# Weight conversions stepped in fewer phases of a pass, and another order of the seven products of a group

## The chip, the cores and the metric

The kernel runs on one core of a Trainium2 chip. The metric is the device time of one execution in microseconds (us). Three runs of the kernel before took 1336.34, 1339.28 and 1339.46 us; the median is 1339.28 us. The engines are called as the profile calls them: PE multiplies matrices (PEld is its weight load), DVE, ACT and POOL work element by element, SP issues the DMAs.

## The reference

Attention over 4 batches of 448 rows and 12 heads of 64, with a normalisation of q and k, and then two feed-forward layers, each of which takes 768 features to 2048 and back. The weights of the layers come as float64.

```
attn   = softmax(rms(q)*g_q @ (rms(k)*g_k).T / 8) @ v       # 4 x 12 x 448 x 64
x      = attn, heads put side by side                        # 1792 x 768
h      = x @ w1_in;  g = s * relu(h)**2 + b;  x = g @ w1_out
h      = x @ w2_in;  g = h * cos(h);          out = g @ w2_out
```

## The kernel before

**The stages.** Attention, and beside it the first layer for batches 0 and 1, fill the first 590 us or so. Then come three passes: the first layer for batches 2 and 3, called (0, 1), the second layer for batches 0 and 1, (1, 0), and for batches 2 and 3, (1, 1). A pass has eight groups p = 0 to 7 (`NCK`), each of 256 of the 2048 hidden features. `phase_in` of a group makes the hidden values, `phase_out` multiplies them with the out-weights and adds to an accumulator. The phases stand in the order in 0, in 1, out 0, in 2, out 1, ..., in 7, out 6, out 7, so that only the first two in-phases of a pass follow each other without an out-phase between them.

**Three matmuls for one product.** Every operand is held as a high and a low part (`halves`, L379: ACT rounds the high part, POOL or DVE subtracts it to get the low one), and `products` (L100) multiplies high by high, low by high and high by low.

**The seven products of a group.** `phase_in` (L743) computes four quarters of the hidden values, two blocks of features by two batches, with seven products instead of eight; sums and differences of weights (`s1` to `s4`, made by `prepare_in`, L685) and of inputs (`1` to `4`, made by `prepare_x`, once for a pass) take the place of the eighth. Each product is 9 matmuls of 128x448 (L763), 63 for a group. Four PSUM banks, a, b, c and d, hold the results:

1. a takes `11` x `11`; ACT copies it out (`p1`, L779).
2. b takes `s2` x `2`; DVE makes `u2` = b + p1 (L767).
3. c takes `s3` x `3`; DVE makes `u3` = c + u2 (L767).
4. d takes `s1` x `1`; DVE adds u3 and writes the quarter (1, 1) to b (L772), and its epilogue starts.
5. a takes on `12` x `21`: quarter (0, 0), no sum needed.
6. c takes on `22` x `4`; DVE adds u2 (L772): quarter (1, 0).
7. d takes on `s4` x `22`; DVE adds u2 (L772): quarter (0, 1).

Product 6 has to wait until u3 has read bank c, product 7 until L772 has read bank d. The epilogue of a quarter (L468 to L483) works in its bank and ends with `gl` (L483) on DVE; only then is the bank free. The next group's four banks are given out in the order in which the group before frees them.

**The conversion of weights.** `convert` (L385) turns one 128x384 piece of float64 weights into float32: SP loads it into one of two `raw` buffers (384 KB), ACT makes `c` and `t` (L402, L403), DVE needs three instructions (L407, L406, L408), SP stores it (L411). The raw buffer is free when L406 has read it. The second layer has 64 such pieces (`pieces`). In passes (0, 1) and (1, 0) every step of a phase adds a fixed rate to a credit (`conversion`, L825), and a piece is converted for each whole credit.

**What sets the order.** The code is written as generators that are stepped side by side, but a scheduler then sets the order of the instructions on each engine by its own timeline: an instruction may stand far ahead of its place in the code if its operands are there. Each engine then works through its list in that order, so an instruction that waits holds up all behind it on its engine.

**Names.** In rows of the order, `u_u2_0_1_6` is u2 of group 6 of pass (0, 1), `ph_1_0_0_a` bank a of group 0 of pass (1, 0), `xr_1_1_...` an input of `prepare_x` for pass (1, 1), `acc` the accumulator (L532 in the first layer, L556 in the second), `c_1_1_7_1_1` and `t_1_1_7_1_1` the working tiles of a converted piece. The DVE's u2 of a group is used as a mark below: "mark 6" is u2 of group 6 of pass (0, 1).

Of the kernel before, what the change touches and what calls it, by code (L numbers as in the profile page):

```python
# [33 lines left out]
def body(ctx, tc, q, k, v, g_q, g_k, w1_in, w1_out, s_in, b_in, w2_in, w2_out, out):  # L34
# [11 lines left out]
    NCK = NF // CF  # L46
# [53 lines left out]
    def products(w, x):  # L100
        return ((w[0], x[0]), (w[1], x[0]), (w[0], x[1]))
# [268 lines left out]
    def tile_of(ck, f):  # L370
        return ck + NCK * f

    def block(key):
        n = count["block"]
        count["block"] += 1
        pool, bufs = (pools["lt"], 5) if "lt" in pools and n % 11 > 5 else (wp, 6)
        return [pool.tile([P, CW], F32R, tag=f"w{z}", name=f"w{z}_{key}", bufs=bufs) for z in "hl"]
# [46 lines left out]
    def recall(key, parts):  # L424
        for z, d in zip(parts, ready[key]):
            nc.sync.dma_start(z.bitcast(F32), d)
# [256 lines left out]
            yield  # L683

    def prepare_in(layer, pr, p):  # L685
        names = ("11", "s2", "s3", "s1", "12", "22", "s4")
        w = late_w["in", layer, pr, p] = {z: block(f"{layer}_{pr}_{p}_{z}") for z in names}
        if (layer, pr) == (1, 1):
            for z in names:
                recall((p, z), w[z])  # L690
                yield
            return

        def fetch(what, f, k):
            nc.sync.dma_start(what, fetched(layer, 0, tile_of(p, f), 0, k))
            return what

        def f32(what):
            return pools["lt"].tile([P, CW], F32, tag="tf", name=f"tf_{layer}_{pr}_{p}_{what}", bufs=4)

        def operand(what, t):
            halves(t, *w[what])
            if layer == 1:
                store((p, what), w[what])

        a11, a22, a12 = (fetch(w[z][1].bitcast(F32), *at) for z, at in (("11", (0, 0)), ("22", (1, 1)), ("12", (0, 1))))
        a21 = fetch(f32("21"), 1, 0)
        yield
        s1, s2 = f32("s1"), f32("s2")
        nc.gpsimd.tensor_tensor(s1, a21, a22, ALU.add)  # L710
        nc.gpsimd.tensor_tensor(s2, s1, a11, ALU.subtract)
        yield
        nc.gpsimd.tensor_tensor(a21, a11, a21, ALU.subtract)
        operand("11", a11)
        yield
        operand("s2", s2)
        yield
        nc.gpsimd.tensor_tensor(s2, a12, s2, ALU.subtract)
        operand("s3", a21)
        yield  # L720
        operand("s1", s1)
        yield
        operand("12", a12)
        yield
        operand("22", a22)
        operand("s4", s2)
        yield
# [15 lines left out]
    def phase_in(layer, pr, p):  # L743
# [12 lines left out]
        def bank(what):  # L756
            return pools["psb"].tile([P, 512], F32, tag="ph", name=f"ph_{key}_{what}", bufs=4)[:, :S]

        def product(at, a, b, first):
            wb = [z.rearrange("p (c f) -> p c f", f=P) for z in w[a]]  # L760
            for c in range(NE // 2):
                for n, (z, m) in enumerate(products([z[:, c, :] for z in wb], x[b, c])):
                    nc.tensor.matmul(at, z, m, start=(first and c == 0 and n == 0), stop=(c == NE // 2 - 1 and n == 2), skip_group_check=not first)  # L763
# [6 lines left out]
        def result(f, b, h, u=None, into=None):  # L770
            if u is not None:
                nc.vector.tensor_tensor(into, h, u, ALU.add)  # L772
                h = into
            epilogue_in_bank(layer, f"{key}_{f}_{b}", h, *(z[:, b, :] for z in pairs[f]))

        pa = bank("a")
# [5 lines left out]
        product(pb, "s2", "2", True)  # L782
        u2 = combine("u2", pb, p1)
        yield
        pc = bank("c")
        product(pc, "s3", "3", True)
        u3 = combine("u3", pc, u2)
# [1 line left out]
        pd = bank("d")  # L789
        product(pd, "s1", "1", True)  # L790
        result(1, 1, pd, u3, pb)
        yield
        product(pa, "12", "21", False)
        result(0, 0, pa)
        yield
        product(pc, "22", "4", False)
        result(1, 0, pc, u2, pc)
# [20 lines left out]
    def fetched(*key):  # L818
        while key not in plain:
            convert(*pieces.pop(0), late=True)  # L820
        return plain[key]
# [3 lines left out]
    def conversion(rate):  # L825
        credit[0] += rate
        while pieces and credit[0] >= 1:
            credit[0] -= 1
            convert(*pieces.pop(0), late=True)
# [45 lines left out]
    passes = [(0, 1), (1, 0), (1, 1)]  # L875
# [12 lines left out]
    for n, (phase, *at) in enumerate(phases):  # L888
        behind = [prepared(phases[n + 1])] if n + 1 < len(phases) else []
        q_, p = tuple(at[:2]), at[2]  # L890
        later = passes[passes.index(q_) + 1:]
        if later and p == NCK - 2 and phase is phase_out:
            soon = [prepare_x(*later[0])]
        for _ in phase(*at):
            for z in behind:
                next(z, None)
            for z in soon:
                next(z, None)
                next(z, None)
            if q_ != passes[-1]:  # L900
                conversion(6 / 13 if q_ == passes[0] else 2.3 / 14)
        for z in behind:
            for _ in z:
                pass
# [28 lines left out]
```

## Time and profile before

| | |
|---|---|
| median of three runs | 1339.28 us |
| the profiled execution | 1341.06 us, of which the span 1339.3 us |
| PE busy in the span | 1231.5 us (92%) |
| DVE busy in the span | 976.0 us (73%) |
| ACT, POOL busy | 778.6 us (58%), 576.5 us (43%) |
| mean granted clock of PE | 0.965 |
| first matmul of pass (0, 1) after a wait | 594.19 us |
| mark 0 and mark 6 of pass (0, 1) on DVE | 617.41 and 792.65 us |
| the first group of pass (1, 0), its u2 | 873.9 us |

A line of a timeline gives the start, the duration, the engine, the line of the kernel, the operation with its output and inputs, and in square brackets the time that the engine had been idle and what ended it. A line of groups gives the busy time in us, the mean of one in ns, and behind the bar the idle time just before such instructions. Matmuls are pipelined, so the time from start to start, not the printed duration, is what one costs.

### The profile page before, as it was taken

The numbers are of one execution on the slowest core, as the hardware profiler recorded it, in microseconds if no ns is written. First come the engines' busy times: TensorE is split into PE (matmuls) and PEld (weight loads), VectorE is DVE, ScalarE is ACT, GpSimd is POOL, SyncE is SP. The second block draws the span as 40 slices with busy tenths as digits, with TensorE's granted clock in tenths as the row PEclk, the third lists the DMA queues.
The fourth block names the chain that finished last, engine by engine and source line by source line (L and its number), as shares of the span: only waits on it lengthen the run. The fifth ranks groups of instructions, "written<-read, shape, count | busy, mean of one in ns | idle before, by whom it ended". The sixth has DMA issues, their size and how long they took to land.

```text
span 1339.3 us, 19446 instructions
## 1 busy us (share of the span) xinstructions
PE 1231.5 (92%) x6408; PEld 1012.5 (76%) x6408; DVE 976.0 (73%) x1539; ACT 778.6 (58%) x1749; POOL 576.5 (43%) x647
## 2 busy tenths in 40 slices
PE   5999998989999899876988999979999979999998
PEld 2555665667677676655977889869999979999997
DVE  5889768677767765899788887665776785566666
ACT  4778768655566554536766656457655644644442
POOL 3666538453353431456333335556555741111120
PEclk9999999999999999886999899989999989999999
DMA  3323325534443331686878776464544637433432
GB/s 101 111 88 120 122 74 173 169 110 133 124 158 103 108 109 57 205 284 206 265 222 255 236 231 206 156 223 154 174 162 137 205 102 236 131 112 112 146 103 83
DMA packets 152069, 207.83 MB, mean 155 GB/s; under 512 B 15872, under 2 KB 141984, under 8 KB 151968
## 3 DMA queue, kind: packets, MB, share of 16 engines
q1 hardware_dynamic: 151968, 206.60, 48.7%
q8 instruction: 50, 0.82, 0.3%
q14 instruction: 51, 0.42, 0.1%
HBM read 139.30 MB, written 67.24 MB: 154 GB/s over the span
## 4 chain that ended last, share of the span: by engine, by line
PE 52%; DVE 17%; ACT 11%; DMA 10%; issue 6%; POOL 4%; SPq 1%; ACTq 0%; POOLq 0%; DVEq 0%
PE po L548 17%; PE po L523 8%; PE ph_a L763 5%; DMA raw<-in_moe_w_in_dram 5%; PE ph_d L763 4%; PE ph_c L763 4%; DVE t L406 4%; ACT pr L230 3%; PE av L271 3%; PE sc L210 3%; PE ph_b L763 3%; PE ph L494 2%; DMA raw<-in_moe_w_out_dram 2%; PE tp L248 2%; DVE t L408 2%
## 5 line engine op out<-in xcount | busy, mean ns | idle before, releaser
L383 POOL TENSOR_TENSOR wl_o<-wl_o,wh_o 128x384 fp32r<-128x384 f32 x64 | 67.0, 1058 | 230.9 <-ACT wh_o L380 214.4
L548 PE MATMUL po<-wh_o,gh 128*128 128x384 f32 x448 | 151.5, 339 | 8.4 <-DVE acc L556 8.4
L230 ACT ACTIVATE pr<-sc,top 112x448 f32<-112x448 f32 x184 | 116.2, 634 | 69.9 <-DVE top L222 69.6
L548 PE MATMUL po<-wh_o,gl 128*128 128x384 f32 x448 | 150.1, 336 | 0.0
L548 PE MATMUL po<-wl_o,gh 128*128 128x384 f32 x448 | 148.5, 336 | 0.0
L402 ACT ACTIVATE c<-raw 128x384 f32<-128x384 f32 x128 | 71.2, 556 | 106.7 <-DMA raw<-in_moe_w_in_dram 46.2
L556 DVE TENSOR_TENSOR acc<-po,acc 128x768 f32<-128x768 f32 x98 | 93.2, 952 | 53.0 <-PE po L548 52.7
L248 PEld LDWEIGHTS tp<-ident,pr 112*112 112x112 f32 x768 | 78.5, 134 | 68.8 <-DVE pT L252 12.9
L222 DVE TENSOR_REDUCE top<-sc 112x1 f32<-112x448 f32 x192 | 112.7, 615 | 23.6 <-PE sc L210 22.8
L532 DVE TENSOR_TENSOR acc<-po,acc 128x448 f32<-128x448 f32 (+1 forms) x126 | 96.8, 772 | 35.9 <-PE po L523 35.7
L406 DVE SCALAR_TENSOR_TENSOR t<-raw,t 128x384 uint32<-128x384 uint32 x128 | 102.4, 801 | 26.5 <-ACT t L403 24.1
L248 PE MATMUL tp<-ident,pr 112*112 112x112 f32 x768 | 102.8, 266 | 12.7 <-ACT pT L254 5.4
L407 DVE TENSOR_SCALAR c<-c 128x384 f32<-128x384 f32 x128 | 69.9, 548 | 59.7 <-ACT c L402 59.4
L210 PE MATMUL sc<-kT,qT 64*112 64x448 f32 x384 | 99.4, 595 | 0.9 <-DVE kT L201 0.9
L408 DVE SCALAR_TENSOR_TENSOR t<-c,t 128x384 uint32<-128x384 uint32 x128 | 93.3, 731 | 1.9
L383 POOL TENSOR_TENSOR wl<-t,wh 128x384 fp32r<-128x384 f32 x64 | 68.3, 1075 | 60.9 <-ACT wh L380 59.6
L548 PEld LDWEIGHTS po<-wh_o,gh 128*128 128x128 f32 x448 | 84.9, 189 | 11.5 <-DVE acc L556 9.8
L523 PE MATMUL po<-gh,wh 128*128 128x448 f32 x192 | 78.0, 407 | 11.4 <-ACT r L459 8.9
L548 PEld LDWEIGHTS po<-wh_o,gl 128*128 128x128 f32 x448 | 84.5, 189 | 1.2
L548 PEld LDWEIGHTS po<-wl_o,gh 128*128 128x128 f32 x448 | 84.4, 189 | 0.3
L710 POOL TENSOR_TENSOR tf_s<-tf,wl 128x384 f32<-128x384 f32 x16 | 17.7, 1104 | 147.0 <-DMA wl<-wd 144.8
L271 PE MATMUL av<-pT,rawv 112*64 112x448 f32 x384 | 79.4, 548 | 0.2 <-DVE pT L252 0.2
(175 smaller groups left out, 3540.4 us busy)
## 6 DMA issues: line engine op xcount, KB each, us to landing
raw<-in_moe_w_in_dram SPq DMA_DIRECT2D x64, 384.0 KB, 3.8
raw<-in_moe_w_out_dram SPq DMA_DIRECT2D x64, 384.0 KB, 3.6
wd<-t SPq DMA_DIRECT2D x96, 192.0 KB, 3.6
wl_o<-wd SPq DMA_DIRECT2D x64, 192.0 KB, 2.4
rd<-wh SPq DMA_DIRECT2D x56, 192.0 KB, 1.9
rd<-wl SPq DMA_DIRECT2D x56, 192.0 KB, 2.3
wl<-wd SPq DMA_DIRECT2D x48, 192.0 KB, 3.2
wh_o<-rd SPq DMA_DIRECT2D x32, 192.0 KB, 3.7
```

The lines of the kernel that those rows point to most:

```text
L210: mm.append(nc.tensor.matmul(sc[j], st[i]["qT"][half, c * CP:(c + 1) * CP], st[i]["kT"][half, :], start=True, stop=True))
L222: line("DVE", nc.vector.tensor_reduce(tops[j], sc[j], axis=AX.X, op=ALU.max, negate=True))
L230: e = line("ACT", nc.scalar.activation(pr, sc[j], AF.Exp, bias=tops[j], scale=scale[j], accum_out=st[i]["sums"][:, c, j:j + 1]))
L248: mm = [nc.tensor.transpose(tp[:, kc * CP:(kc + 1) * CP], pr[:, kc * CP:(kc + 1) * CP], ident[:CP, :CP]) for kc in range(NCH)]
L271: mm.append(nc.tensor.matmul(st[i]["pa"][j * D:(j + 1) * D, :], st[i]["v"][:, j, kc, :], st[i]["pT", j][:, kc, :], start=(kc == 0), stop=( ...
L383: eng.tensor_tensor(wl, w, wh.bitcast(F32), ALU.subtract)
L406: nc.vector.scalar_tensor_tensor(t, hi, 0x80000000, t, ALU.bitwise_and, ALU.bitwise_or)
L408: nc.vector.scalar_tensor_tensor(t, c, 3, t, ALU.logical_shift_left, ALU.bitwise_or)
L523: nc.tensor.matmul(po[:, k, :], a, m, start=(f == 0 and n == 0), stop=(f == CF - 1 and n == 2))
L532: nc.vector.tensor_tensor(at, po, at, ALU.add)
L548: nc.tensor.matmul(po[:, eh, :], a, m, start=(f == 0 and n == 0), stop=(f == CF - 1 and n == 2))
L763: nc.tensor.matmul(at, z, m, start=(first and c == 0 and n == 0), stop=(c == NE // 2 - 1 and n == 2), skip_group_check=not first)
```

## The change

The conversions are stepped in fewer phases: none in the in-phase of group 0 and of group 7, none in the out-phases of groups 6 and 7, and at a higher rate in pass (1, 0) (5/14 of a piece for a step instead of 2.3/14). In `phase_in` the product `12` x `21` moves from fifth to third place, so bank a is finished first. `prepare_in` names and makes the weights in the order of their new use.

```diff
--- before.py
+++ after.py
@@ -683,7 +683,7 @@
             yield
 
     def prepare_in(layer, pr, p):
-        names = ("11", "s2", "s3", "s1", "12", "22", "s4")
+        names = ("11", "s2", "12", "s3", "s1", "22", "s4")
         w = late_w["in", layer, pr, p] = {z: block(f"{layer}_{pr}_{p}_{z}") for z in names}
         if (layer, pr) == (1, 1):
             for z in names:
@@ -716,11 +716,11 @@
         operand("s2", s2)
         yield
         nc.gpsimd.tensor_tensor(s2, a12, s2, ALU.subtract)
+        operand("12", a12)
+        yield
         operand("s3", a21)
         yield
         operand("s1", s1)
-        yield
-        operand("12", a12)
         yield
         operand("22", a22)
         operand("s4", s2)
@@ -782,6 +782,9 @@
         product(pb, "s2", "2", True)
         u2 = combine("u2", pb, p1)
         yield
+        product(pa, "12", "21", False)
+        result(0, 0, pa)
+        yield
         pc = bank("c")
         product(pc, "s3", "3", True)
         u3 = combine("u3", pc, u2)
@@ -789,9 +792,6 @@
         pd = bank("d")
         product(pd, "s1", "1", True)
         result(1, 1, pd, u3, pb)
-        yield
-        product(pa, "12", "21", False)
-        result(0, 0, pa)
         yield
         product(pc, "22", "4", False)
         result(1, 0, pc, u2, pc)
@@ -891,14 +891,15 @@
         later = passes[passes.index(q_) + 1:]
         if later and p == NCK - 2 and phase is phase_out:
             soon = [prepare_x(*later[0])]
+        calm = p >= (phase is phase_in) and (p < NCK - 2 or p == NCK - 2 and phase is phase_in)
         for _ in phase(*at):
             for z in behind:
                 next(z, None)
             for z in soon:
                 next(z, None)
                 next(z, None)
-            if q_ != passes[-1]:
-                conversion(6 / 13 if q_ == passes[0] else 2.3 / 14)
+            if calm:
+                conversion(5.8 / 13 if q_ == passes[0] else 5 / 14)
         for z in behind:
             for _ in z:
                 pass
```

In the order that the scheduler makes of it, the conversions move within pass (0, 1) only. This is the DVE's list from mark 6 on, before:

```order
L767 TENSOR_TENSOR u_u2_0_1_6_8512<-ph_0_1_6_b_8502,u_p1_0_1_6_8490 128x448
L483 TENSOR_TENSOR gl_0_1_5_1_8174<-ph_0_1_5_c_8222,gh_0_1_5_1_8173 128x448
L407 TENSOR_SCALAR c_1_0_15_0_1_11187<-c_1_0_15_0_1_11187 128x384
L532 TENSOR_TENSOR acc_0_1_7112<-po_0_4_2_2_2_8382,acc_0_1_7112 128x896
L406 SCALAR_TENSOR_TENSOR t_1_0_15_0_1_11188<-raw_1_0_15_0_1_11185,t_1_0_15_0_1_11188 128x384
L483 TENSOR_TENSOR gl_0_1_5_0_8172<-ph_0_1_5_d_8236,gh_0_1_5_0_8171 128x448
L408 SCALAR_TENSOR_TENSOR t_1_0_15_0_1_11188<-c_1_0_15_0_1_11187,t_1_0_15_0_1_11188 128x384
L532 TENSOR_TENSOR acc_0_1_7112<-po_0_4_3_2_2_8399,acc_0_1_7112 128x896
L407 TENSOR_SCALAR c_1_1_7_0_0_11328<-c_1_1_7_0_0_11328 128x384
L406 SCALAR_TENSOR_TENSOR t_1_1_7_0_0_11329<-raw_1_1_7_0_0_11326,t_1_1_7_0_0_11329 128x384
L408 SCALAR_TENSOR_TENSOR t_1_1_7_0_0_11329<-c_1_1_7_0_0_11328,t_1_1_7_0_0_11329 128x384
L767 TENSOR_TENSOR u_u3_0_1_6_8537<-ph_0_1_6_c_8527,u_u2_0_1_6_8512 128x448
```

And the DVE's list from mark 6 on, now:

```order
L767 TENSOR_TENSOR u_u2_0_1_6_8468<-ph_0_1_6_b_8458,u_p1_0_1_6_8435 128x448
L407 TENSOR_SCALAR c_1_1_7_1_1_11561<-c_1_1_7_1_1_11561 128x384
L406 SCALAR_TENSOR_TENSOR t_1_1_7_1_1_11562<-raw_1_1_7_1_1_11559,t_1_1_7_1_1_11562 128x384
L408 SCALAR_TENSOR_TENSOR t_1_1_7_1_1_11562<-c_1_1_7_1_1_11561,t_1_1_7_1_1_11562 128x384
L532 TENSOR_TENSOR acc_0_1_7079<-po_0_4_5_2_2_8399,acc_0_1_7079 128x896
L483 TENSOR_TENSOR gl_0_1_6_0_8422<-ph_0_1_6_a_8425,gh_0_1_6_0_8421 128x448
L767 TENSOR_TENSOR u_u3_0_1_6_8509<-ph_0_1_6_c_8499,u_u2_0_1_6_8468 128x448
L772 TENSOR_TENSOR ph_0_1_6_b_8458<-ph_0_1_6_d_8513,u_u3_0_1_6_8509 128x448
L532 TENSOR_TENSOR acc_0_1_7079<-po_0_5_0_2_2_8581,acc_0_1_7079 128x896
```

Before, five conversions (L407, L406, L408 each) stand between mark 6 and mark 7; now one, the last. Mark 7 is the same place in both lists (row 1047), and so is mark 0 (row 787), with the same instructions between them.

The second place is PE at the first group of pass (1, 0), where products 3 and 4 of the list above stood behind each other. Before:

```order
L763 MATMUL ph_1_0_0_c_9451<-xh_1_0_3_2_9287,wh_1_0_0_s3_9154 128x448
L763 MATMUL ph_1_0_0_c_9451<-xh_1_0_3_2_9287,wl_1_0_0_s3_9155 128x448
L763 MATMUL ph_1_0_0_c_9451<-xl_1_0_3_2_9288,wh_1_0_0_s3_9154 128x448
L763 MATMUL ph_1_0_0_d_9470<-xh_1_0_1_0_9026,wl_1_0_0_s1_9157 128x448
L763 MATMUL ph_1_0_0_d_9470<-xl_1_0_1_0_9027,wh_1_0_0_s1_9156 128x448
L763 MATMUL ph_1_0_0_d_9470<-xh_1_0_1_1_9169,wh_1_0_0_s1_9156 128x448
L763 MATMUL ph_1_0_0_d_9470<-xh_1_0_1_1_9169,wl_1_0_0_s1_9157 128x448
```

Now:

```order
L763 MATMUL ph_1_0_0_c_9324<-xh_1_0_3_2_9155,wl_1_0_0_s3_9036 128x448
L763 MATMUL ph_1_0_0_a_9250<-xh_1_0_21_0_8935,wh_1_0_0_12_9033 128x448
L763 MATMUL ph_1_0_0_a_9250<-xh_1_0_21_0_8935,wl_1_0_0_12_9034 128x448
L763 MATMUL ph_1_0_0_a_9250<-xl_1_0_21_0_8936,wh_1_0_0_12_9033 128x448
L763 MATMUL ph_1_0_0_a_9250<-xh_1_0_21_1_9056,wh_1_0_0_12_9033 128x448
L763 MATMUL ph_1_0_0_a_9250<-xh_1_0_21_1_9056,wl_1_0_0_12_9034 128x448
L763 MATMUL ph_1_0_0_a_9250<-xl_1_0_21_1_9057,wh_1_0_0_12_9033 128x448
L763 MATMUL ph_1_0_0_a_9250<-xh_1_0_21_2_9192,wh_1_0_0_12_9033 128x448
L763 MATMUL ph_1_0_0_a_9250<-xh_1_0_21_2_9192,wl_1_0_0_12_9034 128x448
L763 MATMUL ph_1_0_0_a_9250<-xl_1_0_21_2_9193,wh_1_0_0_12_9033 128x448
L763 MATMUL ph_1_0_0_c_9324<-xl_1_0_3_2_9156,wh_1_0_0_s3_9035 128x448
L763 MATMUL ph_1_0_0_d_9342<-xh_1_0_1_0_8927,wl_1_0_0_s1_9038 128x448
```

The nine matmuls of `12` x `21` into bank a stand ahead of those into bank d, and one of bank c behind them.

The third place is DVE in the same group. Before, from u2 on:

```order
L767 TENSOR_TENSOR u_u2_1_0_0_9445<-ph_1_0_0_b_9435,u_p1_1_0_0_9414 128x448
L767 TENSOR_TENSOR u_u3_1_0_0_9461<-ph_1_0_0_c_9451,u_u2_1_0_0_9445 128x448
L663 TENSOR_TENSOR xr_1_1_3_0_11808<-xr_1_1_22_3_11802,xr_1_1_12_0_11800 128x448
L772 TENSOR_TENSOR ph_1_0_0_b_9435<-ph_1_0_0_d_9470,u_u3_1_0_0_9461 128x448
L665 TENSOR_TENSOR xr_1_1_12_0_11800<-xr_1_1_12_0_11800,xr_1_1_11_0_11804 128x448
L668 TENSOR_TENSOR xr_1_1_11_0_11804<-xr_1_1_11_0_11804,xr_1_1_3_0_11808 128x448
L772 TENSOR_TENSOR ph_1_0_0_c_9451<-ph_1_0_0_c_9451,u_u2_1_0_0_9445 128x448
L477 SCALAR_TENSOR_TENSOR gt_1_0_0_1_1_9484<-kk_1_0_0_1_1_9481,ph_1_0_0_b_9435 128x448
L477 SCALAR_TENSOR_TENSOR gt_1_0_0_0_0_9510<-kk_1_0_0_0_0_9507,ph_1_0_0_a_9404 128x448
```

Now:

```order
L767 TENSOR_TENSOR u_u2_1_0_0_9291<-ph_1_0_0_b_9281,u_p1_1_0_0_9260 128x448
L663 TENSOR_TENSOR xr_1_1_3_0_11808<-xr_1_1_22_3_11802,xr_1_1_12_0_11800 128x448
L767 TENSOR_TENSOR u_u3_1_0_0_9334<-ph_1_0_0_c_9324,u_u2_1_0_0_9291 128x448
L665 TENSOR_TENSOR xr_1_1_12_0_11800<-xr_1_1_12_0_11800,xr_1_1_11_0_11804 128x448
L772 TENSOR_TENSOR ph_1_0_0_b_9281<-ph_1_0_0_d_9342,u_u3_1_0_0_9334 128x448
L668 TENSOR_TENSOR xr_1_1_11_0_11804<-xr_1_1_11_0_11804,xr_1_1_3_0_11808 128x448
L477 SCALAR_TENSOR_TENSOR gt_1_0_0_0_0_9309<-kk_1_0_0_0_0_9306,ph_1_0_0_a_9250 128x448
L772 TENSOR_TENSOR ph_1_0_0_c_9324<-ph_1_0_0_c_9324,u_u2_1_0_0_9291 128x448
L478 SCALAR_TENSOR_TENSOR gt_1_0_0_0_0_9309<-kk_1_0_0_0_0_9306,gt_1_0_0_0_0_9309 128x448
```

The subtraction L663, which prepares inputs for pass (1, 1), stood behind u3 and now stands ahead of it; the epilogue of bank a (`gt_1_0_0_0_0`) now stands ahead of that of bank b (`gt_1_0_0_1_1`).

## Rows read from the trace of the kernel before

**Rows 1.** The page, part 1 (share of the span) and the granted clock in 40 slices.
```profile
PE 1231.5 (92%) x6408; PEld 1012.5 (76%) x6408; DVE 976.0 (73%) x1539; ACT 778.6 (58%) x1749; POOL 576.5 (43%) x647
...
PEclk9999999999999999886999899989999989999999
```

**Rows 2.** The busy time by stretch: us, engines (x instructions), PEclk, DMA share, GB/s.
```profile
617.40:792.70 175.30, 153.77 (x684) 136.47 (x685) 147.65 (x225) 119.27 (x248) 72.69 (x64) 0.91 0.77 239
792.70:825.40 32.70, 32.14 (x159) 29.45 (x158) 23.18 (x39) 18.73 (x39) 12.49 (x13) 1.00 0.67 207
825.40:873.90 48.50, 46.47 (x220) 42.15 (x219) 30.51 (x38) 20.25 (x42) 22.14 (x20) 0.96 0.57 193
898.70:1064.00 165.30, 165.28 (x877) 157.33 (x876) 110.47 (x161) 102.42 (x201) 94.06 (x90) 1.00 0.47 159
1096.90:1288.80 191.90, 191.90 (x1022) 183.37 (x1021) 121.59 (x190) 92.44 (x179) 25.50 (x25) 1.00 0.47 148
```

**Rows 3.** The timeline of DVE, start and us: marks of group 0 and group 6.
```profile
617.41 0.61 DVE L767 TENSOR_TENSOR u_u<-ph_b,u_p 128x448 f32<-128x448 f32 x1
...
792.65 0.62 DVE L767 TENSOR_TENSOR u_u<-ph_b,u_p 128x448 f32<-128x448 f32 x1
```

**Rows 4.** The groups of DVE, 617.4 to 792.7: busy, mean ns, idle before.
```profile
L406 DVE SCALAR_TENSOR_TENSOR t<-raw,t 128x384 uint32<-128x384 uint32 x49 | 36.8, 751 | 1.6
...
L408 DVE SCALAR_TENSOR_TENSOR t<-c,t 128x384 uint32<-128x384 uint32 x49 | 35.9, 737 | 0.8
...
L407 DVE TENSOR_SCALAR c<-c 128x384 f32<-128x384 f32 x49 | 27.6, 563 | 21.9 <-ACT c L402 21.8
...
L532 DVE TENSOR_TENSOR acc<-po,acc 128x896 f32<-128x896 f32 x20 | 21.5, 1080 | 0.3 <-PE po L523 0.3
```

**Rows 5.** The tile raw, 617.4 to 792.7: durations, idle ended by, landing.
```profile
L406 DVE SCALAR_TENSOR_TENSOR t<-raw,t x49: 544/558/1415, 619.3 to 791.6; 128x384 uint32<-128x384 uint32 x49
...
  DMA raw<-in_moe_w_in_dram: 26.5, 16
...
DMA to landing us min/median/max: 3.0/3.9/5.9
```

**Rows 6.** The timeline, one turn of a raw buffer, SP and DVE.
```profile
706.04 0.33 SPq L396 DMA_DIRECT2D raw<-in_moe_w_out_dram  x1
...
711.07 0.56 DVE L406 SCALAR_TENSOR_TENSOR t<-raw,t 128x384 uint32<-128x384 uint32 x1
...
711.65 0.33 SPq L396 DMA_DIRECT2D raw<-in_moe_w_out_dram  x1
```

**Rows 7.** The timeline of PE, two matmuls with eight between them.
```profile
867.15 0.37 PE L523 MATMUL po<-gh,wh_o 128*128 128x448 f32 x1
...
869.01 0.37 PE L523 MATMUL po<-gh,wh_o 128*128 128x448 f32 x1
```

**Rows 8.** The timeline of PE, matmuls with the wait before them in brackets.
```profile
631.75 0.74 PE L763 MATMUL ph_a<-xh,wh 128*128 128x448 f32 x1 [6.27 <-DVE gl L483]
...
845.48 0.47 PE L523 MATMUL po<-gh,wh_o 128*128 128x448 f32 x1 [2.03 <-DVE acc L532]
...
892.20 0.74 PE L763 MATMUL ph_a<-xh,wh 128*128 128x448 f32 x1 [9.80 <-DVE gl L483]
...
1085.24 0.69 PE L548 MATMUL po<-wh_o,gh 128*128 128x384 f32 x1 [7.25 <-DVE acc L556]
```

**Rows 9.** The timeline of DVE around the first group of the second layer.
```profile
875.20 0.62 DVE L767 TENSOR_TENSOR u_u<-ph_c,u_u 128x448 f32<-128x448 f32 x1 [0.65 <-PE ph_c L763]
...
877.63 1.50 DVE L663 TENSOR_TENSOR xr<-xr,xr 128x448 f32<-128x448 f32 x1 [1.80 <-DMA xr<-yd]
...
879.05 0.62 DVE L772 TENSOR_TENSOR ph_b<-ph_d,u_u 128x448 f32<-128x448 f32 x1
...
891.53 0.62 DVE L483 TENSOR_TENSOR gl<-ph_b,gh 128x448 fp32r<-128x448 f32 x1
```

**Rows 10.** The timeline of DVE ahead of the wait at 1085.24.
```profile
1084.24 0.94 DVE L556 TENSOR_TENSOR acc<-po,acc 128x768 f32<-128x768 f32 x1
```

## The prediction

> **What bounds the kernel now.** I read the page first: PE is busy for 92% of the span and its granted clock stands at 9 tenths in nearly all slices [rows 1]. So a gain can come only from the 8% in which PE stands still, a loss from new standstills. The busy time by stretch says where these lie. In most of pass (1, 0) (898.70 to 1064.00) and of pass (1, 1) (1096.90 to 1288.80) PE is busy for all but 0.02 us [rows 2]: whatever DVE, ACT and POOL do there is covered, unless it grows into a wait. In pass (0, 1), from mark 0 at 617.41 to mark 6 at 792.65 [rows 3], PE is busy for 153.77 of 175.30 us and DVE for 147.65 [rows 2], so neither is full, and the next view has to say who waits for whom.
>
> The groups of DVE answer that. Of its 175.30 − 147.65 = 27.7 idle us, 21.9 stand ahead of L407 and are ended by ACT's `c`, the first step of a conversion; 0.3 stand ahead of the accumulator L532, for PE [rows 4]. DVE thus hardly waits for PE here; it waits for the next piece of weights. The tile `raw` says why: 26.5 us of idle time were ended by its DMA, a load lands 3.0 to 5.9 us after its issue [rows 5], and SP issues the next load when L406 has read the buffer: issued at 706.04, read at 711.07, the next issued at 711.65, 5.6 us for a turn [rows 6]. With two buffers that is at best 2.8 us for a conversion; 49 conversions [rows 4] in 175.3 us are 3.58 us each. PE waits for what DVE hands on late, as 6.27 us for a `gl` at 631.75 [rows 8]. So until mark 6 the pace is that of DVE with its conversions.
>
> Behind mark 6 the pacer is PE: 32.14 of 32.70 us, then 46.47 of 48.50 [rows 2]. There a matmul costs (869.01 − 867.15) / 9 = 0.2067 us [rows 7].
>
> **The change part by part.** The diff alone reads as if many conversions went to pass (1, 0), where DVE is busy for only 110.47 of 165.30 us [rows 2]. The order shows that none does. All 64 pieces stand ahead of mark 7 in both lists, and from mark 0 to mark 7 DVE has the same 260 instructions, PE the same 848 matmuls. What moves lies between: ahead of mark 6 there are now 53 conversions instead of 49, 3 more L532 and 2 more `gl` (L483); behind it one conversion instead of five, as the first order pieces show. By group (mark 0 to 1, and so on) the conversions were 5, 7, 12, 7, 10, 8 and 5, and are 6, 8, 10, 10, 9, 10 and 1. PE has 36 matmuls more ahead of mark 6 and 36 fewer behind it.
>
> A, mark 0 to mark 6, where DVE is the pacer: a conversion takes 0.751 + 0.737 + 0.563 = 2.05 us of DVE, an L532 1.08 [rows 4], a `gl` 0.62 [rows 9]. So 4 × 2.05 + 3 × 1.08 + 2 × 0.62 = 8.2 + 3.2 + 1.2 = +12.6 us, with DVE's idle time left as it is. Bounds: if the 21.9 us of waiting for `c` take it all in, 0; if a conversion costs its whole share of the stretch, 4 × 3.58 = +14.3 by conversions alone. I take 12.6: with ten conversions in a group of some 29 us (175.3 / 6) a group needs 2.9 us for each, close to the 2.8 of the loop, so evener spacing leaves the loop no more air than before.
>
> L406 took between 0.544 and 1.415 us [rows 5] with POOL busy for 72.69 us of the stretch [rows 2]. The Trainium skill, "SBUF — State Buffer", section "Who interferes with whom", says that a DVE instruction with two inputs from SBUF contends with a GpSimd instruction that reads SBUF. The spread agrees; if the four moved conversions met a quiet POOL, A would be some 2 us less.
>
> B, mark 6 to the end of the pass, where PE is the pacer: 36 × 0.2067 = −7.4 us. The bound on the other side is 0, if what is late there is not PE but the epilogue of group 7.
>
> C, the four conversions that are gone behind mark 6: PE's cover hides them now, except for the 0.56 us of 32.70 − 32.14 [rows 2] and the wait of 2.03 us for `acc` at 845.48 [rows 8]. I take 0, the bound is −2.6.
>
> D, the start of pass (1, 0). PE waits 9.80 us at 892.20 until a `gl` frees a bank [rows 8]; that `gl` starts at 891.53 [rows 9]. Finishing bank a third should free it earlier. Against that stands L663: it waits for a DMA until 877.63 and lasts 1.50 us, while u3 runs at 875.20, ahead of it [rows 9]; now L663 stands ahead of u3 (third order place). Behind L663 on DVE are queued u3, L772 and every epilogue of the group, and product 6 on PE waits for u3 to read bank c. u3 would end at about 879.05 + 0.62 = 879.7 instead of 875.8, where product 4 of the list is through at about 879.0. So some 1 us of new wait stands against an epilogue of bank a that follows at once: I come to a `gl` that ends between 891.3 and 892.1, as now. Value 0; bounds −4 (the epilogue goes ahead by the 3.7 us of two products of nine matmuls) and +3 (the wait for L663 comes on top).
>
> E, the start of pass (1, 1): PE waits 7.25 us at 1085.24 for an accumulator step [rows 8] that starts at 1084.24 [rows 10], DVE being full ahead of it. Between this step and the one of the block before, DVE's list has one L477, one L478 and one L483 fewer and one L481 more now: about −1, bounds −3 and +2.
>
> F, the other groups of (1, 0) and (1, 1). Product 6 has to wait for u3, product 7 for L772; until now product 5 lay between, 9 × 0.2067 = 1.9 us of cover. Now only the product just ahead covers it. u3 takes 0.62 us [rows 9] once DVE is free, and matmuls of the out-phase stand between in PE's list. Value 0 on PE's 165.28 of 165.30 us [rows 2]; the bound is +12, from 14 groups at 0.9 us (the longest DVE instruction in the way lasts 1.50 [rows 9], less 0.6 left of cover). The making of `12` ahead of `s3` on POOL costs nothing: POOL is busy for 43% of the span [rows 1].
>
> Sum: 12.6 − 7.4 + 0 + 0 − 1 + 0 = +4.2 us on the profiled 1341.06 us, 1345.3. The median of the runs is 1.8 us below that execution: 1343.5 us.
>
> **The rivals.** First, faster: the bank. Bank a is done first now, and the next group's first product takes it. If its epilogue gets through DVE at once, the waits between groups shrink: 9.80 us at 892.20, and in pass (0, 1) those like the 6.27 at 631.75 [rows 8]. With 5 us of the one, 3 of the 7.25, and A lowered to 4 by the hand-over in pass (0, 1): 4 − 7.4 − 5 − 3 = −11, about 1328 us. For it: the waits exist and are ended by `gl`. Against it: in pass (0, 1) DVE is the pacer, so PE's waiting is not the price; and L663.
>
> Second, no change: evener spacing lets the loop hide. If about a quarter of the 21.9 us [rows 4] goes, A is 12.6 − 5.5 = 7.1, the sum −1.3, 1338 us. For it: before, groups of 12 and of 5 conversions stood side by side. Against it: the 2.8 us of the loop.
>
> Third, clearly slower: products 6 and 7 without their cover. It decides if DVE is behind by more than 1.9 us when product 4 of the list ends. At 0.9 us in 14 groups it adds 12 to part of the sum: with A at its value and the rest, 4.2 + 12 = 16; with half of the groups, +10, so about 1350 to 1355 us. For it: DVE instructions of 1.50 us stand in the list; against it, DVE is busy for only 110.47 of 165.30 and 121.59 of 191.90 us there [rows 2].
>
> That the conversions do move into pass (1, 0) is a rival too: pass (0, 1) would then run at PE's pace, 848 × 0.2067 = 175 us instead of 208 (175.30 + 32.70 [rows 2]) from mark 0 to mark 7, about 1306 us. The Trainium skill, "Perfetto Trace Analysis", section "Optimization Strategy", says that interleaving stretches with different bottlenecks may help, which speaks for such a move. The lists exclude it: no conversion stands behind mark 7.
>
> **How the numbers follow.** Forecast, a small loss (1338 to 1349 us by its own terms: A between 7 and 14.3, D and E by 3 either way): 0.53. The bank: 0.20. No change by spacing: 0.12. Lost cover: 0.15. A measurement of this kernel tells some 0.3% from no change, 4 us: 1335.3 to 1343.3. Faster: the bank's 0.19 and 0.04 of spacing, 0.23. Same: the lower part of the forecast, 0.25, spacing 0.08 and 0.01 of the bank, 0.34. Slower: the rest, 0.28 and 0.15, 0.43. The range takes in the bank's value and the near part of the lost cover: 1328 to 1352 us.
>
> **What would show it.** In the new profile mark 6 should come some 12 us later against mark 0 (some 188 us instead of 175.3), and mark 7 some 5 us later; DVE's idle time ahead of L407 about 22 us; the waits at the starts of the two last passes as now within 3 us. Wrong, if mark 6 comes less than 6 us later or the idle time falls well below 20 (spacing), if the wait at the start of (1, 0) falls below 6 us (the bank), or if PE shows waits for `u_u` or `ph_b` in most groups behind 900 us (cover).

## The result: 0.6% slower, and the profile after

Seven runs of the changed kernel took 1343.12 to 1348.72 us, median 1345.69, against 1338.52 us of the kernel before in the same measurement. The ratio is 1.0061, interval 1.0043 to 1.0078. The profiled execution has a span of 1345.7 us. The page's first part, for the changed kernel:

```profile
PE 1229.1 (91%) x6408; PEld 1008.1 (75%) x6408; DVE 978.1 (73%) x1539; ACT 784.6 (58%) x1749; POOL 578.7 (43%) x647
```

Every engine runs as many instructions as in [rows 1], and PE is busy 2.4 us less; so the loss lies in standstills of PE. The same stretches as in [rows 2], from the changed kernel (us, then busy time and instructions of PE, PEld, DVE, ACT, POOL, clock, DMA share, GB/s):

```profile
617.00:806.60 189.60, 158.89 (x721) 139.72 (x722) 156.38 (x241) 123.98 (x257) 73.90 (x64) 0.94 0.75 238
806.60:831.60 25.00, 25.00 (x125) 23.17 (x124) 15.12 (x21) 15.15 (x30) 13.16 (x13) 1.00 0.46 145
831.60:879.60 48.00, 45.86 (x217) 41.61 (x216) 31.13 (x39) 20.83 (x42) 21.74 (x19) 0.96 0.54 188
903.30:1069.10 165.80, 162.48 (x859) 154.05 (x858) 110.06 (x161) 102.31 (x201) 95.84 (x91) 1.00 0.47 157
1106.70:1291.50 184.80, 184.80 (x985) 176.85 (x984) 118.75 (x185) 94.12 (x175) 25.13 (x24) 1.00 0.48 151
```

From mark 0 to mark 6 it is 189.6 us instead of 175.3 [rows 2], from mark 6 to mark 7 25.0 instead of 32.7, on to the first group of (1, 0) 48.0 instead of 48.5. The marks 0, 6 and 7 on DVE, as in [rows 3]:

```profile
616.96 0.61 DVE L767 TENSOR_TENSOR u_u<-ph_b,u_p 128x448 f32<-128x448 f32 x1
...
806.64 0.61 DVE L767 TENSOR_TENSOR u_u<-ph_b,u_p 128x448 f32<-128x448 f32 x1
...
831.64 0.61 DVE L767 TENSOR_TENSOR u_u<-ph_b,u_p 128x448 f32<-128x448 f32 x1
```

The groups of DVE from mark 0 to mark 6 (busy, mean ns, idle before), as in [rows 4]:

```profile
L406 DVE SCALAR_TENSOR_TENSOR t<-raw,t 128x384 uint32<-128x384 uint32 x53 | 40.1, 757 | 1.6
L408 DVE SCALAR_TENSOR_TENSOR t<-c,t 128x384 uint32<-128x384 uint32 x53 | 37.7, 716 | 0.9
L407 DVE TENSOR_SCALAR c<-c 128x384 f32<-128x384 f32 x53 | 28.6, 540 | 30.3 <-ACT c L402 30.2
L532 DVE TENSOR_TENSOR acc<-po,acc 128x896 f32<-128x896 f32 x23 | 24.8, 1081 | 0.0
```

The waits of PE that answer to [rows 8]: the one at the start of group 1 (two matmuls of group 0's out-phase now stand there), one behind mark 7, the starts of (1, 0) and (1, 1).

```profile
635.57 0.71 PE L523 MATMUL po<-gh,wh_o 128*128 128x448 f32 x1 [10.31 <-DMA wh_o<-rd]
...
851.13 0.47 PE L523 MATMUL po<-gh,wh_o 128*128 128x448 f32 x1 [2.14 <-DVE acc L532]
...
896.52 0.74 PE L763 MATMUL ph_a<-xh,wh 128*128 128x448 f32 x1 [6.51 <-DVE gl L483]
...
1091.68 0.69 PE L548 MATMUL po<-wh_o,gh 128*128 128x384 f32 x1 [3.17 <-DVE acc L556]
```

By the marks the forecast seems confirmed step by step: +14.3 for +12.6, −7.7 for −7.4, +6.4 in the span for +4.2. The experiments show that the largest step was right only as book-keeping: the sum came out, the reason given for it didn't hold.

**A measure that doesn't depend on DVE.** A mark is an instruction of DVE, and how far PE has got by then differs between kernels. So PE's lateness is used from here on: the start of the last matmul of product 2 in a group, less that in group 0 of pass (0, 1), less the matmuls between them in PE's list times 0.2067 us [rows 7]. It holds PE's waits and also what matmuls lose at a lower granted clock; its mean from mark 0 to mark 6 was 0.91 before [rows 2] and is 0.94 now. For mark 1, the two matmuls in the kernel before and in the changed one:

```profile
610.37 0.36 PE L763 MATMUL ph_b<-xl,wh_s 128*128 128x448 f32 x1
...
637.99 0.37 PE L763 MATMUL ph_b<-xl,wh_s 128*128 128x448 f32 x1
```

```profile
609.76 0.37 PE L763 MATMUL ph_b<-xl,wh_s 128*128 128x448 f32 x1
...
641.65 0.37 PE L763 MATMUL ph_b<-xl,wh_s 128*128 128x448 f32 x1
```

With 50 and 52 matmuls between them, 27.62 − 10.34 = 17.3 us before and 31.89 − 10.75 = 21.1 now. Worked out so for all kernels (us of lateness; "(1, 0)" is that pass's first group):

| kernel | ratio to before (interval) | mark 1 | mark 2 | mark 6 | mark 7 | (1, 0) |
|---|---|---|---|---|---|---|
| before | 1 | 17.3 | 17.3 | 38.2 | 38.4 | 41.8 |
| changed | 1.0061 (1.0043 to 1.0078) | 21.1 | 23.3 | 45.1 | 44.5 | 48.0 |
| e1 new order, old rates | 1.0054 (1.0034 to 1.0074) | 21.6 | 24.7 | 47.4 | 47.4 | 48.7 |
| e2 new order in (0, 1) only | 1.0068 (1.0041 to 1.0095) | 20.9 | 23.7 | 47.2 | 46.6 | 47.9 |
| e3 new order in (1, 0), (1, 1) only | 1.0001 (0.9984 to 1.0018) | 17.8 | 17.8 | 37.6 | 37.5 | 38.7 |
| e4 five conversions behind mark 6 | 1.0078 (1.0049 to 1.0106) | 21.5 | 25.9 | 46.7 | 47.1 | 52.3 |
| e5 out-phase held back | 1.0041 (1.0023 to 1.0059) | 20.9 | 25.1 | 46.2 | 46.2 | 48.1 |
| e6 group 0 cleared, new order | 1.0028 (1.0011 to 1.0044) | 17.6 | 20.1 | 40.0 | 44.3 | 46.3 |
| e11 group 0 cleared, old order | 1.0000 (0.9988 to 1.0012) | 12.1 | 13.2 | 31.5 | 36.0 | 43.0 |
| e12 old order in group 0 only | 1.0014 (1.0001 to 1.0027) | 17.3 | 20.2 | 39.8 | 41.6 | 43.0 |
| e7 pinned, old order and rates | 0.9886 (0.9859 to 0.9912) | 10.3 | 14.9 | 15.1 | 15.1 | 23.9 |
| e9 pinned, new order, old rates | 0.9882 (0.9862 to 0.9901) | 12.1 | 12.4 | 16.1 | 19.3 | 26.4 |
| e8 pinned, new order, new rates | 0.9964 (0.9949 to 0.9979) | 13.1 | 12.7 | 21.6 | 21.6 | 25.6 |
| e10 pinned, old order, 7/13 and 3/14 | 1.0103 (1.0083 to 1.0123) | 8.6 | 9.6 | 23.4 | 27.1 | 28.0 |

The changed kernel has its whole loss, 6.0 us, by mark 2, and keeps it: 48.0 − 41.8 = 6.2 at the first group of (1, 0). Each row is one execution. The changed kernel and e1 have the same lists (see below), and they differ by up to 2.9 us in a column, so smaller differences than that say little; at mark 1 the five kernels with six conversions in group 0 lie within 0.7 us.

### The profile page after: what moved, and what is told of

Its sections match the earlier page's. It is cut to its first block, busy times and chain, and to the rows that moved or that the text cites. A ratio compares the mean times of both kernels' runs of the same rounds, so it can differ in the third digit from the quotient of the medians.

```text
span 1345.7 us, 19429 instructions
## 1 busy us (share of the span) xinstructions
PE 1229.1 (91%) x6408; PEld 1008.1 (75%) x6408; DVE 978.1 (73%) x1539; ACT 784.6 (58%) x1749; POOL 578.7 (43%) x647
## 3 DMA queue, kind: packets, MB, share of 16 engines
q1 hardware_dynamic: 151968, 206.60, 47.9%
## 4 chain that ended last, share of the span: by engine, by line
PE 47%; DVE 20%; ACT 11%; DMA 10%; issue 6%; POOL 5%; SPq 0%; POOLq 0%; ACTq 0%; DVEq 0%
PE po L548 15%; PE po L523 8%; DMA raw<-in_moe_w_in_dram 5%; DVE t L406 5%; PE ph_a L763 4%; ACT pr L230 4%; PE av L271 3%; PE ph_c L763 3%; PE sc L210 3%; PE ph_d L763 3%; PE ph L494 2%; DVE t L408 2%; PE ph_b L763 2%; PE tp L248 2%; DMA raw<-in_moe_w_out_dram 2%
## 5 line engine op out<-in xcount | busy, mean ns | idle before, releaser
L402 ACT ACTIVATE c<-raw 128x384 f32<-128x384 f32 x128 | 71.3, 557 | 101.7 <-DMA raw<-in_moe_w_in_dram 41.6
L222 DVE TENSOR_REDUCE top<-sc 112x1 f32<-112x448 f32 x192 | 112.8, 616 | 23.7 <-PE sc L210 22.9
L532 DVE TENSOR_TENSOR acc<-po,acc 128x448 f32<-128x448 f32 (+1 forms) x126 | 97.0, 773 | 38.0 <-PE po L523 37.6
L406 DVE SCALAR_TENSOR_TENSOR t<-raw,t 128x384 uint32<-128x384 uint32 x128 | 103.6, 810 | 26.1 <-ACT t L403 23.9
L407 DVE TENSOR_SCALAR c<-c 128x384 f32<-128x384 f32 x128 | 69.6, 545 | 64.0 <-ACT c L402 63.6
L248 PE MATMUL tp<-ident,pr 112*112 112x112 f32 x768 | 102.6, 266 | 13.2 <-ACT pT L254 5.3
L523 PE MATMUL po<-gh,wh_o 128*128 128x448 f32 x192 | 73.8, 386 | 25.5 <-DVE acc L532 13.7
L408 DVE SCALAR_TENSOR_TENSOR t<-c,t 128x384 uint32<-128x384 uint32 x128 | 92.5, 726 | 1.9
```

Of the source, the lines that this page charges most:

```text
L222: line("DVE", nc.vector.tensor_reduce(tops[j], sc[j], axis=AX.X, op=ALU.max, negate=True))
L248: mm = [nc.tensor.transpose(tp[:, kc * CP:(kc + 1) * CP], pr[:, kc * CP:(kc + 1) * CP], ident[:CP, :CP]) for kc in range(NCH)]
L406: nc.vector.scalar_tensor_tensor(t, hi, 0x80000000, t, ALU.bitwise_and, ALU.bitwise_or)
L408: nc.vector.scalar_tensor_tensor(t, c, 3, t, ALU.logical_shift_left, ALU.bitwise_or)
L523: nc.tensor.matmul(po[:, k, :], a, m, start=(f == 0 and n == 0), stop=(f == CF - 1 and n == 2))
L532: nc.vector.tensor_tensor(at, po, at, ALU.add)
```

## The experiments

In the edits, `...` stands for lines left out. A `gate` is an instruction of ACT behind which the two ACT steps of a conversion have to issue.

**e1: the product order without the conversions' new rates.** The pieces of the diff on products and weights stay, the last one is undone:

```
...
-            if calm:
-                conversion(5.8 / 13 if q_ == passes[0] else 5 / 14)
+            if q_ != passes[-1]:
+                conversion(6 / 13 if q_ == passes[0] else 2.3 / 14)
```

> The new order of products with the old conversion rates and phases. The lists of every engine are those of the changed kernel, row for row. Theory (the whole effect comes through the product order, because the scheduler places the conversions by its own timeline): 1345 to 1346 us, mark 6 some 189.6 us behind mark 0, as in the changed kernel. Rival (the rates and the calm phases are half of the effect): about 1342 us.

Measured: 1344.88 us, and nearly the lateness of the changed kernel. The half of the change that is about conversions does nothing: the scheduler makes the same lists from either rate, on all five engines.

**e2 and e3: the new order in one layer's passes.** In e3 the conditions are reversed; `prepare_in` likewise.

```
...
+        if layer == 0:
+            product(pa, "12", "21", False)
+            result(0, 0, pa)
+            yield
         pc = bank("c")
...
+        if layer != 0:
+            product(pa, "12", "21", False)
+            result(0, 0, pa)
+            yield
```

> The new product order in the first layer's pass (0, 1) only; passes (1, 0) and (1, 1) have the old one. Pass (0, 1) has the changed kernel's DVE list, the later passes that of the kernel before. Theory (the loss is made in pass (0, 1), by four conversions that stand ahead of mark 6): 1345 us, mark 6 189 to 190 us behind mark 0, mark 7 some 214.5 us, and from u2 of the first group of (1, 0) to the end 465.4 us as before. Rival (lost cover of products 6 and 7 in the two last passes): 1339 to 1341 us.

> The new product order in passes (1, 0) and (1, 1) only. Theory: within 1.5 us of the kernel before, since the waits that shrink at the starts of the passes (about 4 us) are spent on new waits of 0.5 to 1.4 us between them. Rival (lost cover): 5 us or more slower. Second rival (the bank freed first): 3 us or more faster.

Measured: 1347.61 and 1337.98 us. The loss is made in pass (0, 1). In the two last passes the order is neutral as far as 12 runs can tell (0.9984 to 1.0018); both rivals there fall.

**e4: five conversions behind mark 6 again.** The gate is the first epilogue instruction of a quarter of group 6.

```
...
+    def gate_of():
+        n = 63 - len(pieces)
+        return epi_of.get('0_1_6_0_0') if n >= 59 else None
...
-            convert(*pieces.pop(0), late=True)
+            convert(*pieces.pop(0), gate=gate_of(), late=True)
```

> The changed kernel, with its last five conversions held back until ACT starts the epilogue of group 6 of pass (0, 1): 49 conversions ahead of mark 6 and five behind, as in the kernel before, everything else in DVE's list as in the changed kernel. Theory (a conversion ahead of mark 6 costs DVE's time, one behind it is covered by PE): mark 6 comes 8 us earlier than in the changed kernel (181 to 182 us behind mark 0), the part from mark 6 to mark 7 stays at 25 to 26 us, the time is 1337 to 1340 us. Rival (the loss is PE's wait of 10.3 us in group 0 and the product order itself, not the conversions): mark 6 at 187 us or more, 1343 to 1346 us.

Measured: 1347.59 us, no gain. The marks 0, 6 and 7 of this kernel on DVE:

```profile
618.13 0.61 DVE L770 TENSOR_TENSOR u_u<-ph_b,u_p 128x448 f32<-128x448 f32 x1
...
804.96 0.61 DVE L770 TENSOR_TENSOR u_u<-ph_b,u_p 128x448 f32<-128x448 f32 x1
...
838.14 0.62 DVE L770 TENSOR_TENSOR u_u<-ph_b,u_p 128x448 f32<-128x448 f32 x1
```

Mark 6 comes 186.8 us behind mark 0, 2.8 earlier than in the changed kernel and not 8; the stretch to mark 7 grows from 25.0 to 33.2. PE's lateness at mark 6 is 46.7, near the changed kernel's 45.1 and e1's 47.4. So the edit moved DVE's mark against PE's work, not PE. The theory on which the forecast's first two terms rest falls here: both its mark and its time are missed. The rival comes nearer, but isn't met either: 186.8 where it had 187 or more, 1347.59 where it had 1343 to 1346. Whether its reason is right is the next run's question.

**e5: PE's order at the change from group 0 to group 1.** In PE's new list two out-phase matmuls stand ahead of group 1's first product, and PE waits with them until 635.57 (above).

```
...
+                    if pr == 1 and ck == 0 and k == f == n == 0:
+                        issue_after(z, product_end["0_1_1", "s2"])
...
```

> The changed kernel, with the first out-phase matmuls of group 0 of pass (0, 1) held back on PE behind the second product of group 1. In the changed kernel two of them stand ahead of group 1's first product and PE waits with them until 635.6 us, for out-weights that SP loads late; bank a is free at 634.2. Theory (the loss is made at the change from group 0 to group 1, by PE's order): PE starts group 1 some 2 us earlier, the time falls by 2 us or a little more to 1342 to 1344 us. Rival (the first groups are late because DVE and ACT have more to do ahead of the banks' release, whatever PE's order): PE waits for a gl instead, to within 1 us of the same moment, 1345 to 1347 us.

Measured: 1345.07 us, lateness at mark 1 unchanged: the rival. PE now waits for a `gl` to nearly the same moment:

```profile
634.85 0.74 PE L766 MATMUL ph_a<-xh,wh 128*128 128x448 f32 x1 [8.40 <-DVE gl L484]
```

What that `gl` waits for is in the timelines of ACT and DVE. In the kernel before, ACT's `gh` of the bank that is freed first, and the `gl` that ends its use:

```profile
627.36 0.55 ACT L482 CAST gh<-ph_b 128x448 fp32r<-128x448 f32 x1
...
631.08 0.62 DVE L483 TENSOR_TENSOR gl<-ph_b,gh 128x448 fp32r<-128x448 f32 x1
```

In the changed kernel the same two, and ahead of them the last matmul of that bank on PE:

```profile
624.69 0.37 PE L763 MATMUL ph_a<-xl,wh 128*128 128x448 f32 x1
...
632.96 0.57 ACT L482 CAST gh<-ph_a 128x448 fp32r<-128x448 f32 x1
...
633.61 0.62 DVE L483 TENSOR_TENSOR gl<-ph_a,gh 128x448 fp32r<-128x448 f32 x1
```

Before, group 1's first product took over bank b, free at 631.70; now it takes over bank a, free at 634.23. In this one group, bank a is not done early though its product is written third: its last matmul, on an input that `prepare_x` makes at that time, runs at 624.69, when all else of the group but one matmul is through.

**e6 and e11: fewer conversions in group 0, in the new order and in the old.** The gate is `gh`, the last ACT step of the epilogue, of the last quarter of group 0.

```
...
+        n = 63 - len(pieces)
+        return gh_of.get('0_1_0_0_1') if n >= 11 else None
...
```

> The changed kernel, with conversions from the twelfth on held back on ACT behind the last epilogue of group 0 of pass (0, 1): two conversions fewer between mark 0 and mark 1 (4 instead of 6), and no out-phase matmul ahead of group 1's first product in PE's list. Theory (group 0's end sets the loss; conversions there stand in ACT's and DVE's lists ahead of the epilogue of bank a): PE's lateness at mark 1 falls by 3 to 4 us, the time to 1340 to 1342 us. Rival (the number of conversions in the whole pass sets the time, wherever they stand): no gain, 1345 us or more.

> The kernel before, with conversions from the twelfth on held back on ACT behind the last epilogue of group 0: one conversion instead of five between mark 0 and mark 1, nine instead of five behind mark 6, all else in DVE's list as before. It is the control to the same edit in the new order, which gave back 3.5 us of PE's lateness at mark 1. Theory (conversions ahead of the banks' release in group 0 cost PE's time, whatever the product order): lateness at mark 1 falls from 17.3 us to 13 to 15; the end gains 2 to 4 us, unless nine conversions in group 6 give it back. Rival (in the old order the bank freed first is b, whose epilogue stands ahead of the conversions, so there is nothing to gain): 17 us at mark 1 as before.

Measured: 1342.79 and 1339.83 us. In both, lateness at mark 1 falls, by 3.5 and 5.2 us (e11's theory had 2.3 to 4.3). e6's time misses its theory by 0.8 us; in e11 the end gains nothing, as its theory allowed for if the conversions behind mark 6 give the gain back. PE starts group 1 earlier, here in e6, behind the last matmul of product 2 in group 0:

```profile
610.27 0.36 PE L764 MATMUL ph_b<-xl,wh_s 128*128 128x448 f32 x1
...
632.28 0.74 PE L764 MATMUL ph_a<-xh,wh 128*128 128x448 f32 x1 [6.50 <-DVE gl L484]
```

The same two in e11:

```profile
607.58 0.36 PE L764 MATMUL ph_b<-xl,wh_s 128*128 128x448 f32 x1
...
625.73 0.48 PE L764 MATMUL ph_a<-xh,wh 128*128 128x448 f32 x1 [1.25 <-DVE gl L484]
```

In both, a single conversion stands on DVE between mark 0 and the `gl` that ends PE's wait. With as many conversions in the way, the new order still starts group 1 later, 632.28 − 610.27 = 22.0 us behind product 2 and not 625.73 − 607.58 = 18.2. So the order costs some 4 us at this place with the conversions equal, and conversions ahead of the release cost PE in either order.

The control in the old order tells more: its gain of 6.7 us at mark 6 (38.2 − 31.5) shrinks to 2.4 at mark 7, behind the stretch in which the four conversions now stand, and is gone at the first group of (1, 0). These four conversions moved within the pass moved their cost. So e6 alone doesn't explain the loss: the edit helps the early groups of either order.

**e12: the old order in group 0 alone.** All other groups of all passes keep the new one; `prepare_in` and the product's old place likewise.

```
...
+        if (layer, pr, p) != (0, 1, 0):
+            product(pa, "12", "21", False)
+            result(0, 0, pa)
+            yield
...
```

> The changed kernel with the old product order in one group alone, group 0 of pass (0, 1). Theory (the loss is made at the change from group 0 to group 1, where the new order hands on bank a, freed at 634.2 us, instead of bank b, freed at 631.7): PE's lateness at mark 1 is 15 to 17.5 us as in the kernel before, at the first group of (1, 0) 41 to 44, and the time is 1337 to 1341 us. Rival (the new order costs in every group of the pass, or the five conversions that again stand behind mark 6 cost there what group 0 gives back): lateness 45 us or more at the first group of (1, 0), 1343 us or more.

Measured: 1340.49 us, lateness 17.3 at mark 1 and 43.0 at the first group of (1, 0), both as the theory says. PE starts group 1 when it did in the kernel before, at 631.75 [rows 8]:

```profile
631.83 0.74 PE L767 MATMUL ph_a<-xh,wh 128*128 128x448 f32 x1 [4.67 <-DVE gl L483]
```

The order in one group of 24 holds 0.47 of the 0.61% (1.0061 to 1.0014; the intervals don't meet). Two things change with it in the lists. Five conversions stand behind mark 6, as in e4; e4, with the new order in group 0, gained nothing. And four instead of six stand in group 0, as in e6; at mark 1, 2 and 6 the lateness of e12 is that of e6 within 0.3 us. So e12 alone doesn't tell the bank from these two conversions; e6 beside e11 does, and there the order counts with the conversions equal. How the 0.47 divides between the two isn't shown. The rest, 1.0014 with an interval from 1.0001, and the 2.9 us that still arise between mark 1 and mark 2, are not traced to an instruction; every kernel that isn't pinned loses 2.2 to 4.4 us there with the new order in group 1, and 0 to 1.1 with the old.

**e7 to e10: conversions that can't be hoisted.** In these, each late conversion is held on ACT behind the last `gh` or `p1` written ahead of it.

```
...
+    def gate_of():
+        return last_act[0]
...
-            convert(*pieces.pop(0), late=True)
+            convert(*pieces.pop(0), gate=gate_of(), late=True)
```

> The kernel before (old product order, old rates), with every late conversion held on ACT behind the epilogue instruction written ahead of it in the code, so that the scheduler can't hoist it: 38 conversions between mark 0 and mark 7 instead of 54, 16 in pass (1, 0) and one in (1, 1). Theory (in pass (0, 1) DVE and the conversion loop keep PE waiting, in (1, 0) they don't): the stretch from mark 0 to mark 7 falls by 20 to 30 us, pass (1, 0) loses up to 5, the time is 1312 to 1325 us. Rival (as in the run with five conversions behind mark 6, conversions are off PE's path): 1335 us or more.

> The changed kernel (new product order, new rates and calm phases) with every late conversion held on ACT behind the epilogue instruction written ahead of it, so that the written rates count: 32 conversions between mark 0 and mark 7, 30 in pass (1, 0). It is what the text of the change says. Theory: pass (0, 1) runs near PE's pace (175 us for its 848 matmuls, some 185 to 190 with the changes of group), pass (1, 0) loses 5 to 10 us because DVE gets 30 x 2.05 = 62 us more beside 110 of 165; 1310 to 1325 us. Rival: 1335 us or more.

> The pinned kernel with the old rates (1323.4 us in the old product order), in the new product order. Nothing can be hoisted, so the order's effect shows without a shift of conversions. Theory (the new order costs only through conversions that the scheduler puts ahead of the banks' release in the first groups): within 3 us of 1323.4. Rival (the new order itself keeps PE waiting in every pass): 1329 us or more. The difference between the two pinned kernels already run (1323.4 and 1334.4) would then be the rates' by the theory, because 30 conversions in pass (1, 0) are too many for DVE, and the order's by the rival.

> Old product order, pinned, the calm phases of the change, at 7/13 in pass (0, 1) and 3/14 in (1, 0): about seven conversions in each group from 2 to 6, one in group 7, 20 behind. In the pinned run with the old rates PE's lateness stayed at 15 us from group 2 to group 7 with six in a group, and rose to 24 in group 7, where it had nine, and its span was 1323.8 us. Theory (DVE has room for seven, not for nine beside the out-phases of groups 6 and 7): 1315 to 1321 us. Rival (three to six conversions in the groups of (1, 0) cost as much as group 7 gives back): 1322 to 1330 us.

Measured: 1323.41, 1334.41, 1323.20 and 1353.96 us. Two of them, e7 and e9, beat the kernel before by 1.1 to 1.2%. Mark 0 and u2 of the first group of (1, 0) in e7:

```profile
603.79 0.62 DVE L769 TENSOR_TENSOR u_u<-ph_b,u_p 128x448 f32<-128x448 f32 x1
...
846.07 0.61 DVE L769 TENSOR_TENSOR u_u<-ph_b,u_p 128x448 f32<-128x448 f32 x1
```

Against the kernel before (617.41 [rows 3] and 873.9) it is 13.6 us ahead at mark 0, where the ten conversions that stood ahead of mark 0 are gone, and gains another 14.2 us by the first group of (1, 0); 12.3 are given back in the two last passes (span 1323.8 against 1339.3). The time of e7 is in its theory's range, but the theory had up to 5 us for what pass (1, 0) gives back. e9 has the new order: where nothing can be hoisted, it costs nothing in the time that these runs can tell (1323.20 and 1323.41, intervals 0.9862 to 0.9901 and 0.9859 to 0.9912), though at mark 1 PE is 12.1 us late and not 10.3. e8, at 1334.41 between its theory's 1325 and its rival's 1335, then is slower through its rates: with 30 conversions in pass (1, 0) instead of 17, lateness rises by 25.9 us from that pass's first group to the next pass's (25.6 to 51.5), against 4.8 in e9 (26.4 to 31.2).

e10 was missed by both theories. Group 7 behaves as expected (27.1 to 28.0), but the last conversions come so late in (1, 0) that PE waits for the weights made of them; the waits of PE in this kernel from 594 us on (total, times, longest):

```profile
PE ph_b L765 <- ACT wh_s L382: 15.6, 2, 13.7
PE po L550 <- DVE acc L558: 14.1, 8, 6.3
PE ph_a L765 <- DVE gl L485: 10.6, 2, 10.4
```

The longest, 13.7 us, is ended by the rounding of a weight (`wh_s`).

## Why the prediction was right

**The time** was right: 1343.5 us forecast, 1345.69 measured, slower as forecast, inside 1338 to 1349. The loss itself was forecast too small: 4.2 us, against 6.4 between the spans and 1345.69 − 1338.52 = 7.2 between the medians.

**What moves** was right: no conversion left the pass, in the lists of either kernel, and e1 shows that the rates play no part. The rival in which they do move was rightly excluded; e8 is what it would have been, 1334 us and not 1306, because 30 conversions are more than pass (1, 0) covers.

**A and B** had the right sums (+14.3 and −7.7 against +12.6 and −7.4) by the wrong mechanism; that the sums came out is luck. In A's working, DVE's busy time was to grow by 12.6 us and its idle time not at all; the busy time grew by 156.38 − 147.65 = 8.7 and the idle time by 5.5 (27.7 to 33.2), with 30.3 us ahead of L407 where some 22 were to stay. Above all, the step "mark 0 to mark 6, where DVE is the pacer", by which a conversion more ahead of mark 6 is time lost, failed: e4 takes four conversions away there and the end doesn't come earlier. Those of group 0 do cost PE, but e11 lost behind mark 6 what it had gained by moving them. Half of A's +14.3 is where the mark lies in PE's work: the 36 matmuls more ahead of mark 6 are 7.4 us, which B gives back; the other 45.1 − 38.2 = 6.9 are PE's lateness. What made most of that is the change from group 0 to group 1, where the new order hands on a bank that is free 2.5 us later (e12, and e6 beside e11), with what follows until mark 2, whose cause stays open.

**C** was right: the wait of 2.03 us is still there, with 2.14.

**D** was right: L663 does wait, until 884.07, u3 follows, and product 6 waits for it, in this timeline of DVE and then PE:

```profile
884.07 1.43 DVE L663 TENSOR_TENSOR xr<-xr,xr 128x448 f32<-128x448 f32 x1 [3.90 <-DMA xr<-yd]
...
885.43 0.61 DVE L767 TENSOR_TENSOR u_u<-ph_c,u_u 128x448 f32<-128x448 f32 x1
...
886.09 0.47 PE L763 MATMUL ph_c<-xh,wh 128*128 128x448 f32 x1 [1.79 <-DVE u_u L767]
```

With the 6.51 us for `gl` that is 8.3 us instead of 9.80: −1.5, where 0 stood with −4 to +3.

**E** was too small: the wait of 7.25 us at the start of (1, 1) is now 3.17, −4.1 where −1 stood with a bound of −3. **F** was right within its bounds: in (1, 0) PE has new waits of 165.80 − 162.48 = 3.3 us. Of all waits behind 900 us one is for `u_u`, 1.4 us; the sign of the lost cover, such waits in most groups, is absent. Together D, E and F cancel: from the first group of (1, 0) to the end it is 466.1 us (1345.7 − 879.6) against 465.4, and e3 measures no difference.

**The bank rival** was wrong in sign where it mattered: in the first group of pass (0, 1) the bank written to be done first is free later. It had been weighed with the right waits, 6.27 us among them, and the wrong assumption that a product written earlier is finished earlier.

## What to carry to other kernels

Where a scheduler sets the order, a rate written in the source may not reach the lists at all: compare the lists first, and pin what must not be hoisted (here 1.1%). A stretch between two marks on one engine says nothing of another that runs ahead or behind; count that engine's own work at the marks. And when a product is moved so that its buffer comes free earlier, look for the one group in which its inputs are late: here the old order in that group alone took back three quarters of the loss.

## What was not expected of the hardware

The durations that the profile gives for DVE's instructions overlap. Four `gl` in a row in e6 take 0.61 to 0.62 us each and start 0.53 to 0.54 apart:

```profile
631.60 0.62 DVE L484 TENSOR_TENSOR gl<-ph_a,gh 128x448 fp32r<-128x448 f32 x1 [3.76 <-ACT gh L483]
632.14 0.61 DVE L484 TENSOR_TENSOR gl<-ph_b,gh 128x448 fp32r<-128x448 f32 x1
632.67 0.61 DVE L484 TENSOR_TENSOR gl<-ph_c,gh 128x448 fp32r<-128x448 f32 x1
633.20 0.61 DVE L484 TENSOR_TENSOR gl<-ph_d,gh 128x448 fp32r<-128x448 f32 x1
```

So a sum of durations counts some 15% too much of such a row of instructions. How much of A this is isn't shown; over half of the 3.9 us by which DVE's busy time stayed behind A's 12.6 is that the three rows of the conversions grew by 3.3 + 1.8 + 1.0 = 6.1 us and not by 8.2.
